# Two state-space convolutions and two feed-forward layers on one core: first load of h, warm-up, last store and instruction order changed

## The chip, the cores and the metric

The kernel runs on one core of a Trainium2 chip. The metric is the device time of one execution in microseconds; the verdict of a comparison is the median over several executions.

## The reference

Two layers, each a convolution block A and a feed-forward block B, on 2048 rows of 512 columns in bfloat16. `q` is the running `x`, and each block is added to it.

```python
def _A_ref(q, k, v, shift_k, ssm_k, ssm_D):           # q is layernorm(x)
    k_shift = sum over t of k_pad[:, t:t + S, :] * shift_k[:, ks - 1 - t]   # 4 taps along the rows
    kv = k_shift * v
    y = irfft(rfft(kv, 2S) * rfft(ssm_k, 2S))[:S]     # causal convolution along the rows, 2048 long
    return q * (y + kv * ssm_D)
def _B_ref(x, w_gate, w_up, w_down):                  # x is layernorm(x); 512 -> 1792 -> 512
    return (silu(x @ w_gate) * (x @ w_up)) @ w_down
x = A_q
x = x + A(layernorm(x)); x = x + B(layernorm(x))      # twice, with the same weights
```

## The kernel before

The 2048 rows are cut into four chunks of 512 (`c` = 0 to 3), each laid out as 128 partitions times four rows. The convolution of each chunk works on spectra of length 1024: matmuls with cosine and sine tables (`fwd`) make the spectra `X` of `k_shift * v` and `H`, `G` of the filter, VectorE multiplies them into `Z`, and matmuls with the transposed tables (`inv`) bring them back as `Y`. The taps of `k` are matmuls with diagonal matrices `dg`. `prologue` multiplies `Y` with the normalised `x`, adds, normalises again and turns the result into `zT`. `ffn` runs one unit of 256 rows: gate and up matmuls of 256 columns into PSUM tiles `pf` (line 311), silu and copy on ScalarE into `sg` and `ht` (lines 970 and 974), their product on VectorE (line 977), and the down matmuls into `pd` (line 990). There are 16 units; `LAST_UNIT` is the last.

Nothing is issued as the code stands. `add` records each operation with its engine, a cost, and its predecessors; `Plan.order` sorts the recorded operations by a table of numbers, `ORDER`, written out by hand, and works out starts from the costs and from the latencies (`lat`) given to transfers. `Plan.issue` emits them in that order on the five engines. Where PE would sit idle in the first 32 us by these starts, `issue` puts warm-up matmuls `wm` there through `warm`: so many as fit in the hole at 0.106 us each. They write to a free PSUM buffer and nothing reads them. Each engine keeps its list in order, so that an operation waits behind all that stand ahead of it.

The start goes like this. On ScalarE's queue the taps (`tapR`) and `ssm_D` (`drow`, line 1069, after VectorE's memset of line 1053) are loaded, then the table load and the two `Sin` activations that make `fwd` (line 1105). On SP's queue stand `hn` (`load_h`, the first 512 columns of the filter), `kn` (`load_k`), `vt` (`load_v`), `xc` (`load_x`), the next `hn` and `vt`, and the gate weights. PE turns `hn` (`transpose_h`, line 477) and `kn` (`transpose_k`, line 366); ScalarE and VectorE copy them out as `hs` and `kTb` (lines 487, 490, 493, 372, 374). Spectra of `h` are the eight first matmuls of line 311, copied out as `ev`; `G` follows from `ev` (lines 445 and 447).

`ln_stats_act` takes the sums of a layer norm on ScalarE (lines 828 and 834, with the row sums accumulated beside) for eight of the 32 norms; its last operation on that engine makes `ve`, the variance with the epsilon, which GpSimd raises to the power of -0.5. `ln_stats` does the same with VectorE's `bn_stats` (line 809) and its `ve` on VectorE (line 812).

The last row of the last unit is split by columns into two halves, so that VectorE adds one half (line 1008) and SP stores it while ScalarE copies the other (line 1011) and its own queue stores that (line 1014). For the second half `x` itself is added in PSUM by a matmul with the identity (line 949).

Of the kernel before, what the change touches and what calls it, by code (L numbers as in the profile page):

```python
# [30 lines left out]
LK0 = 4.3  # L31
# [11 lines left out]
H_SPLIT = False  # L43
# [7 lines left out]
LASTV = True  # L51
ORDER = [
# [186 lines left out]
def kernel(  # L239
# [1024 lines left out]
    def warm(ring, slot, n):  # L1264
        t = psp.tile([P, P], F32, name="wm", tag=f"{ring}{slot}")
        for _ in range(n):
            nc.tensor.matmul(t[:], lhsT=wz.t[:], rhs=wz.t[:], start=True, stop=True)  # L1267
# [33 lines left out]
```

## Time and profile before

| what | value |
|---|---|
| time, median of 3 runs | 346.92 us (344.28 to 723.23) |
| the profiled execution: time, span from first to last instruction | 344.93 us, 343.2 us |
| PE busy | 336.4 us (98%), 2579 matmuls |
| PE weight loads | 248.6 us (72%) |
| VectorE busy | 283.4 us (83%), 482 instructions |
| ScalarE busy | 253.9 us (74%), 504 instructions |
| GpSimd busy | 35.3 us (10%) |
| first gate matmul starts | 33.58 us |
| last copy out of PSUM starts | 340.00 us |
| mean granted clock | 1.000 |

Busy time of PE is modelled from starts and does not tell whether matmuls run at full rate; the distance from start to start does. A line of the timeline has the start in microseconds from the first instruction, the duration of the whole group, the engine, the line of the code, what is written from what, the shape and the count, and in brackets the idle time before with what ended it.

### The profile page before, as it was taken

The numbers are of one execution on the slowest core, as the hardware profiler recorded it, in microseconds if no ns is written. First come the engines' busy times: TensorE is split into PE (matmuls) and PEld (weight loads), VectorE is DVE, ScalarE is ACT, GpSimd is POOL, SyncE is SP. The second block draws the span as 40 slices with busy tenths as digits, with TensorE's granted clock in tenths as the row PEclk, the third lists the DMA queues.
The fourth block names the chain that finished last, engine by engine and source line by source line (L and its number), as shares of the span: only waits on it lengthen the run. The fifth ranks groups of instructions, "written<-read, shape, count | busy, mean of one in ns | idle before, by whom it ended". The sixth has DMA issues, their size and how long they took to land.

```text
span 343.2 us, 6553 instructions
## 1 busy us (share of the span) xinstructions
PE 336.4 (98%) x2579; PEld 248.6 (72%) x2610; DVE 283.4 (83%) x482; ACT 253.9 (74%) x504; POOL 35.3 (10%) x46
## 2 busy tenths in 40 slices
PE   8999999999999999999999999999999999999996
PEld 7756868768687676858586777768685877777783
DVE  8899999899999999899999999989998433726022
ACT  6999999899997765958789995779475464446261
POOL 4010100203111000103110100201101001000000
PEclk9999999999999999999999999999999999999999
DMA  7999218310116044040101014210101100110101
GB/s 273 336 316 341 52 27 112 77 32 0 34 31 94 14 95 138 2 94 3 32 2 46 2 46 79 76 32 1 32 0 33 35 13 0 39 39 8 24 26 37
DMA packets 42088, 22.95 MB, mean 67 GB/s; under 512 B 33861, under 2 KB 39882, under 8 KB 42058
## 3 DMA queue, kind: packets, MB, share of 16 engines
q1 hardware_dynamic: 41904, 22.47, 26.6%
q8 instruction: 20, 0.33, 0.4%
q14 instruction: 10, 0.08, 0.1%
q10 hardware_dynamic: 154, 0.07, 0.1%
HBM read 12.33 MB, written 2.10 MB: 42 GB/s over the span
## 4 chain that ended last, share of the span: by engine, by line
PE 91%; ACT 4%; DVE 3%; issue 1%
PE pf L311 54%; PE pd L990 28%; PE ps L311 6%; PE ps L458 1%; ACT H L419 1%; PE wm L1267 1%; DVE bnst L809 1%; ACT hs L487 1%; PE pt L477 1%; ACT X L419 0%; ACT n L859 0%; PE pt L366 0%; DVE m L540 0%; DVE t L665 0%; DVE Z L667 0%
## 5 line engine op out<-in xcount | busy, mean ns | idle before, releaser
L311 PE MATMUL pf<-zT,wu_sb 128*128 128x256 bf16 x896 | 110.4, 273 | 0.1
L311 PE MATMUL pf<-zT,wg_sb 128*128 128x256 bf16 x896 | 110.2, 273 | 0.2
L990 PE MATMUL pd<-wd_sb,ht 128*128 128x512 bf16 (+1 forms) x440 | 102.4, 372 | 1.2
L311 PEld LDWEIGHTS <-wu_sb 128*128 128x128 bf16 x896 | 87.7, 98 | 16.4
L311 PEld LDWEIGHTS <-wg_sb 128*128 128x128 bf16 x896 | 87.6, 98 | 16.5 <-issue 0.8
L974 ACT CAST ht<-pf 128x512 bf16<-128x512 f32 x112 | 64.0, 591 | 29.3 <-PE pf L311 29.1
L970 ACT ACTIVATE sg<-pf 128x512 bf16<-128x512 f32 x112 | 65.5, 603 | 17.4 <-PE pf L311 15.1
L990 PEld LDWEIGHTS <-ht 128*128 128x128 bf16 x462 | 45.2, 98 | 42.5
L977 DVE TENSOR_TENSOR ht<-ht,sg 128x1024 bf16<-128x1024 bf16 (+1 forms) x64 | 39.0, 617 | 24.0 <-ACT sg L970 18.7
L814 POOL TENSOR_TENSOR rstd<-ve,nhalf 128x2 f32<-128x2 f32 x24 | 23.0, 958 | 217.8 <-DVE ve L812 207.6
L1034 ACT CAST dn<-pd 128x512 bf16<-128x512 f32 x30 | 17.0, 589 | 21.0 <-PE pd L990 20.9
L809 DVE BATCH_NORM_STATS2 bnst<-xc 128x6 f32<-128x512 bf16 x48 | 31.6, 684 | 0.6
L419 ACT ACTIVATE X<-ps 128x512 bf16<-128x512 f32 x32 | 19.2, 611 | 4.0 <-PE ps L311 3.4
L653 DVE TENSOR_TENSOR t<-X,G 128x2048 bf16<-128x2048 bf16 x18 | 21.9, 1218 | 0.1
L657 DVE TENSOR_TENSOR t<-X,G 128x2048 bf16<-128x2048 bf16 x18 | 21.9, 1216 | 0.0
L1037 DVE TENSOR_TENSOR xc<-xc,dn 128x1024 bf16<-128x1024 bf16 x15 | 10.3, 689 | 13.4 <-ACT dn L1034 13.2
L665 DVE TENSOR_TENSOR t<-t,t 128x2048 bf16<-128x2048 bf16 x12 | 14.7, 1222 | 0.3
L667 DVE TENSOR_TENSOR Z<-Z,t 128x2048 bf16<-128x2048 bf16 x12 | 14.6, 1220 | 0.2
L840 POOL TENSOR_TENSOR rstd<-ve,nhalf 128x2 f32<-128x2 f32 x8 | 8.7, 1088 | 59.2 <-ACT ve L838 59.1
L419 ACT ACTIVATE H<-ps 128x512 bf16<-128x512 f32 x24 | 13.8, 610 | 0.1
L886 DVE TENSOR_TENSOR n<-n,Yk 128x1024 bf16<-128x1024 bf16 x15 | 10.3, 688 | 4.1 <-ACT n L859 3.8
L604 ACT ACTIVATE kc<-kTb,tapF 128x512 bf16<-128x512 bf16 x16 | 12.1, 783 | 0.0
(105 smaller groups left out, 323.3 us busy)
## 6 DMA issues: line engine op xcount, KB each, us to landing
hn<-in_A_ssm_k_dram SPq DMA_DIRECT2D x4, 512.0 KB, 4.1
vt<-in_A_v_dram SPq DMA_DIRECT2D x4, 512.0 KB, 5.9
xc<-in_A_q_dram SPq DMA_DIRECT2D x4, 512.0 KB, 5.3
out_dram<-xc SPq DMA_DIRECT2D x15, 128.0 KB, 1.8
wg_sb<-in_B_w_gate_dram SPq DMA_DIRECT2D x1, 1792.0 KB
wu_sb<-in_B_w_up_dram SPq DMA_DIRECT2D x1, 1792.0 KB, 8.5
wd_sb<-in_B_w_down_dram SPq DMA_DIRECT2D x1, 1280.0 KB, 12.0
kn<-in_A_k_dram SPq DMA_DIRECT2D x1, 512.0 KB, 4.5
```

Source lines behind the costliest of these rows:

```text
L311: nc.tensor.matmul(o, lhsT=lhsT, rhs=rhs, start=(n == 0), stop=(n == len(terms) - 1))
L419: add("ACT", act(D), lambda: nc.scalar.activation(out=view(), in_=ps.t[:], func=ACT.Copy, scale=scale), r=[ps], w=[(buf, keys)], conv=conv)
L653: dve(n * D, lambda t1=t1, part=part: nc.vector.tensor_mul(out=t1.t[:], in0=x.t[:, sl, 0, :], in1=g.t[:, sl, part, :]), [(x, key(slots, (0 ...
L657: dve(n * D, lambda t2=t2, part=part: nc.vector.tensor_mul(out=t2.t[:], in0=x.t[:, sl, 1, :], in1=g.t[:, sl, 1 - part, :]), [(x, key(slots ...
L665: dve(n * D, lambda t1=t1, t2=t2, comb=comb: nc.vector.tensor_tensor(out=t1.t[:], in0=t1.t[:], in1=t2.t[:], op=comb), [t2], [t1], conv=conv)
L809: add("DVE", 0.6, lambda st=st, i=i: nc.vector.bn_stats(out=st.t[:], in_=xs[c].t[:, i, :]), r=[(xs[c], (i,))], w=[st])
L814: add("POOL", pw, lambda: nc.gpsimd.tensor_tensor(out=rstd.t[:], in0=ve.t[:], in1=nhalf.t[:].to_broadcast((P, n)), op=ALU.pow), r=[ve, nha ...
L970: add("ACT", act(D), lambda ps=ps, o=o, sg=sg: nc.scalar.activation(out=sg.t[:, o:o + 2, :], in_=ps.t[:], func=ACT.Silu), r=[ps], w=[(sg, ...
L974: add("ACT", act(D), lambda ps=ps, o=o, ht=ht: nc.scalar.copy(out=ht.t[:, o:o + 2, :], in_=ps.t[:]), r=[ps], w=[(ht, (o // 2,))], due=(uni ...
L977: dve(n * W, lambda sg=sg, ht=ht: nc.vector.tensor_mul(out=ht.t[:], in0=ht.t[:], in1=sg.t[:]), [sg], [ht], due=(unit, k / pairs, 0.0, "h"))
L990: nc.tensor.matmul((pds[o] if not cs.start else pds[HP]).t[:, cs], lhsT=ht.t[:, q, o * P:(o + 1) * P], rhs=wt["d"].t[:, ft, cs], start=(ft ...
L1034: add("ACT", act(D), lambda o=o: nc.scalar.copy(out=dn.t[:, o, :], in_=pds[o].t[:]), r=[pds[o]], w=[(dn, (o,))], due=(unit, 1.0, 3.0, "h"))
```

## The change

1. `H_SPLIT` is now true: the first `hn` is loaded by two transfers of two blocks each, the second recorded after the first, both ahead of `kn` on SP's queue. PE's transposes of it are then recorded by halves, each waiting for its own transfer.
2. The warm-up matmuls read the framework's constant tile of ones; the tile `wz` and its memset are gone. The number of matmuls in a hole is counted without the 0.3 us that was left free, where the hole begins after 0 and before 8 us, and from 0 for the first one. There are 37 in place of 31: 25 before the taps, 6 between `h` and `k`, 6 ahead of the transposes of `z`.
3. The last row is cut at column 320: VectorE and SP take 320, ScalarE and its queue 192.
4. `ve` in `ln_stats_act` is made by VectorE (`VE_D`): eight operations move.
5. The latencies given to the first `k`, `v` and `x` loads are smaller; they steer the planner's starts alone.
6. `ORDER` is another table throughout. Of what the change speaks of, the lists then stand as follows. PE: 25 `wm`, the four transposes of the taps, 6 transposes of the first half of `h`, 10 that need the second, 6 `wm`, all 16 of `k`, 8 spectrum matmuls (before: 22 `wm`, taps, 5 `wm`, 16 of `h`, 8 of `k`, 8 spectrum matmuls, 8 of `k`). VectorE: `nhalf`, one `ph`, then the memset of `drow`; all eight of its `dg` before its two `kTb` copies. SP: the second `xc` behind both parts of `wd_sb`, where it stood between them.

```diff
-LK0 = 4.3
+LK0 = 3.8
-H_SPLIT = False
+H_SPLIT = True
+TAIL = 320
+VE_D = True
 ORDER = [
...
-                            n = int((start - max(t, 0.3) - 0.3) / 0.106)
+                            n = int((start - t - (0.0 if 0.0 < t < 8.0 else 0.3)) / 0.106)
...
         if b == 0 and H_SPLIT:
+            o = None
             for n in range(2):
                 sl = slice(2 * n, 2 * n + 2)
                 o = add(eng, 0.5, lambda sl=sl: q.dma_start(out=hn[b].t[:, sl], in_=h3[:, sl, 0:L]), w=[(hn[b], (n,))],
-                        lat=LH0 - 0.75 if n == 0 else LH0 - 0.45, due=due, after=after)
+                        lat=(2.95, 3.1)[n], due=due, after=[o] if n else after)
...
-lat=(6.6, 9.0)[b] if b < 2 else 5.5
+lat=(5.7, 8.6)[b] if b < 2 else 5.5
-lat=(7.5, 13.0, 5.0, 5.0)[c]
+lat=(6.2, 13.0, 5.0, 5.0)[c]
...
-        add("ACT", TINY, lambda: nc.scalar.activation(out=ve.t[:], in_=sm.t[:, n:2 * n], func=ACT.Identity, scale=1.0 / D, bias=eps.t[:]),
-            r=[(sm, range(n, 2 * n)), eps], w=[ve])
+        if VE_D:
+            add("DVE", 0.08, lambda: nc.vector.tensor_scalar(out=ve.t[:], in0=sm.t[:, n:2 * n], scalar1=1.0 / D, scalar2=LN_EPS,
+                                                             op0=ALU.mult, op1=ALU.add), r=[(sm, range(n, 2 * n))], w=[ve])
...
-                halves = (slice(0, D // 2), slice(D // 2, D)) if unit == LAST_UNIT and o == HP - 1 else (slice(0, D),)
+                halves = (slice(0, TAIL), slice(TAIL, D)) if unit == LAST_UNIT and o == HP - 1 else (slice(0, D),)
...
-            for half_, (eng, cs) in enumerate((("DVE", slice(0, D // 2)), ("ACT", slice(D // 2, D)))):
+            for half_, (eng, cs) in enumerate((("DVE", slice(0, TAIL)), ("ACT", slice(TAIL, D)))):
...
-    wz = whole("wz", [P, P])
-    add("DVE", 0.07, lambda: nc.vector.memset(wz.t[:], 0.5), w=[wz], due=-80)
+    ones = nc.const_aps.tensor(1.0, (P, P), BF16)
...
-            nc.tensor.matmul(t[:], lhsT=wz.t[:], rhs=wz.t[:], start=True, stop=True)
+            nc.tensor.matmul(t[:], lhsT=ones, rhs=ones, start=True, stop=True)
```

More of the change, by code (lines that the diff above doesn't have):

```diff
@@ L381, in load_v @@
             return add("ACT", 0.45, lambda: nc.scalar.dma_start(out=vt[b].t[:], in_=v_t[:, b]), w=[vt[b]], lat=5.5, due=-69.5, after=[h0])
-        return add("SP", 0.6, lambda: nc.sync.dma_start(out=vt[b].t[:], in_=v_t[:, b]), w=[vt[b]], lat=(6.6, 9.0)[b] if b < 2 else 5.5, due=due, after=after)
+        return add("SP", 0.6, lambda: nc.sync.dma_start(out=vt[b].t[:], in_=v_t[:, b]), w=[vt[b]], lat=(5.7, 8.6)[b] if b < 2 else 5.5, due=due, after=after)
     def load_x(c, due=None, after=()):
         xs[c] = new("x", "xc", [P, R, D], parts=R + 2)
-        return add("SP", 0.7, lambda: nc.sync.dma_start(out=xs[c].t[:], in_=q_t[:, c]), w=[xs[c]], lat=(7.5, 13.0, 5.0, 5.0)[c], due=due, after=after)
+        return add("SP", 0.7, lambda: nc.sync.dma_start(out=xs[c].t[:], in_=q_t[:, c]), w=[xs[c]], lat=(6.2, 13.0, 5.0, 5.0)[c], due=due, after=after)
     def load_weights(which, due, after=()):
@@ L837, in ln_stats_act @@
         ve, rstd = new("ve", "ve", [P, n], F32), new("rs", "rstd", [P, n], F32)
-        add("ACT", TINY, lambda: nc.scalar.activation(out=ve.t[:], in_=sm.t[:, n:2 * n], func=ACT.Identity, scale=1.0 / D, bias=eps.t[:]),
-            r=[(sm, range(n, 2 * n)), eps], w=[ve])
+        if VE_D:
+            add("DVE", 0.08, lambda: nc.vector.tensor_scalar(out=ve.t[:], in0=sm.t[:, n:2 * n], scalar1=1.0 / D, scalar2=LN_EPS,
+                                                             op0=ALU.mult, op1=ALU.add), r=[(sm, range(n, 2 * n))], w=[ve])
+        else:
+            add("ACT", TINY, lambda: nc.scalar.activation(out=ve.t[:], in_=sm.t[:, n:2 * n], func=ACT.Identity, scale=1.0 / D, bias=eps.t[:]),
+                r=[(sm, range(n, 2 * n)), eps], w=[ve])
         add("POOL", PWA, lambda: nc.gpsimd.tensor_tensor(out=rstd.t[:], in0=ve.t[:], in1=nhalf.t[:].to_broadcast((P, n)),
@@ L982, in ffn @@
                 split = unit == LAST_UNIT and o == HP - 1
-                halves = (slice(0, D // 2), slice(D // 2, D))
+                halves = (slice(0, TAIL), slice(TAIL, D))
                 cols = [[cs] for cs in halves] if last else [halves] if split else [[slice(0, D)]]
@@ L991, in go @@
                                                  start=(ft == 0 and not own(o, cs)), stop=(ft == NF - 1))
-                    add("PE", pe(n) if not last else pe(n, D // 2), go, r=[ht, (wt["d"], (0 if fts[0] == 0 else 1,))],
+                    add("PE", pe(n) if not last else pe(n, css[0].stop - css[0].start), go, r=[ht, (wt["d"], (0 if fts[0] == 0 else 1,))],
                         w=[pds[o]] if not split else [pds[o], pds[HP]] if not last else [pds[HP if css[0].start else o]],
@@ L1004, in ffn @@
                 due=(unit, 1.0, 20.0, None))
-            for half_, (eng, cs) in enumerate((("DVE", slice(0, D // 2)), ("ACT", slice(D // 2, D)))):
+            for half_, (eng, cs) in enumerate((("DVE", slice(0, TAIL)), ("ACT", slice(TAIL, D)))):
                 copy = nc.scalar.copy if eng == "ACT" else nc.vector.tensor_copy
                 if LASTV and not half_:
-                    add(eng, 0.35, lambda cs=cs: nc.vector.tensor_add(out=x.t[:, i, cs], in0=x.t[:, i, cs], in1=pds[o].t[:, cs]),
+                    add(eng, 0.42, lambda cs=cs: nc.vector.tensor_add(out=x.t[:, i, cs], in0=x.t[:, i, cs], in1=pds[o].t[:, cs]),
                         r=[pds[o], (x, (i,))], w=[(x, (R + half_,))], due=(unit, 1.0, 3.0, "h"))
                 else:
-                    add(eng, 0.35, lambda cs=cs, copy=copy, half_=half_: copy(out=x.t[:, i, cs], in_=pds[HP if half_ else o].t[:, cs]),
+                    add(eng, 0.3, lambda cs=cs, copy=copy, half_=half_: copy(out=x.t[:, i, cs], in_=pds[HP if half_ else o].t[:, cs]),
                         r=[pds[HP if half_ else o]], w=[(x, (R + half_,))], due=(unit, 1.0, 3.0, "h"))
```

116 rows, old and new, of the table ORDER are left out of this document.

## The prediction

> **What bounds the kernel now.** I read the page's slices first, then PE's waits over the whole span, then the order of time at both ends.
>
> ```profile
> span 343.2 us, 6553 instructions
> PE   8999999999999999999999999999999999999996
> DVE  8899999899999999899999999989998433726022
> PEclk9999999999999999999999999999999999999999
> ```
>
> The second list is the waits of PE: who released it, then us in total, times, longest.
>
> ```profile
> PE wm L1267 <- DVE wz L1050: 1.0, 1, 1.0
> PE ps L311 <- ACT H L419: 0.4, 1, 0.4
> PE ps L311 <- DVE vt L515: 0.4, 1, 0.4
> ```
>
> The two waits for `H` and `vt` fall at 24 and 31 us. The first gate matmul (`pf`) starts at 33.58 us, and PE waits for nothing it could be given after that. The chain shows the rate:
>
> ```profile
> 303.27 10.48 PE pf L311 x96
> 317.23 3.45 PE pd L990 x16
> ```
>
> That is 109 ns per 256 columns and 216 ns per 512. From 33.58 us to the last matmul at about 340 us TensorE runs one matmul after the other at that rate, so a new order can gain nothing there; it can only open holes. What can be gained lies ahead of 33.58 us and behind 340 us. First column start, second duration:
>
> ```profile
> 0.72 0.45 SPq L342 DMA_DIRECT2D hn<-in_A_ssm_k_dram  x1
> 0.82 0.17 DVE L1050 MEMSET wz<- 128x128 bf16 x1 [0.82 <-PEq L1285]
> 1.04 2.53 PE L1267 MATMUL wm<-wz 128*128 128x128 bf16 x22 [1.04 <-DVE wz L1050]
> 1.24 0.48 SPq L352 DMA_DIRECT2D kn<-in_A_k_dram  x1
> 3.50 0.29 PE L1133 MATMUL pt<-ident,tapR 4*128 4x4 bf16 x4
> 4.49 1.86 PE L477 MATMUL pt<-ident,hn 128*128 128x128 bf16 x16
> 6.15 1.06 PE L366 MATMUL pt<-ident,kn 128*128 128x128 bf16 x8
> 8.87 0.61 PE L366 MATMUL pt<-ident,kn 128*128 128x128 bf16 x8
> ```
>
> Sixteen transposes of `h` take 1.86 us, each starting 107 ns after the one before; the second eight of `k` start 56 ns apart. So TensorE runs at half its clock until the first columns of L311 at about 7.3 us and at full clock from then on. The PEclk row shows 9 throughout and hides this; the spacing is the measure.
>
> Work ahead of 33.58 us at full rate: 48 transposes of `h` and `k`, 8 of `z` and 128 matmuls of `dg` at 56 ns are 10.3 us, 74 matmuls of 512 columns at 216 ns are 16.0 us, together 26.3 us. From 4.49 us that would end at 30.8. So 2.8 us are lost there: 24 transposes at 107 in place of 56 ns (1.2 us), a half-rate matmul (0.1), the two waits (0.8), and small steps. VectorE matters just as much: its idle times in that stretch are these, and from 10 us on it has almost none.
>
> ```profile
> DVE kTb L374 <- PE pt L366: 1.2, 2, 0.6
> DVE G L447 <- ACT ev L419: 0.4, 1, 0.4
> ```
>
> **The change, part by part.**
>
> First `h` in two transfers: one more SP issue of 0.45 us. The first half, 256 KB, cannot land sooner than a 4 KB transfer nor later than the whole: `tapR`, issued at 0.72, is used at 3.49 (2.8 us), the whole `h` lands 3.6 us after issue. That is 3.5 to 4.3 us; I take 3.7. PE's list does six transposes of the first half, then ten that need the second. The second half is issued at about 1.2; its bytes are behind the same bytes as before, so I take 4.3, with 4.8 (3.6 after its own issue) as the late end. The ten at 107 ns then end at 5.5 (6.0 late) where 6.2 was the end: 0.2 to 0.7 us earlier. `k`, `v`, `x` and all else on SP's queue are issued 0.45 us later; `k` landed 4.5 us after issue, at 5.7, and would land at 5.7 if its bytes wait for those of `h` anyway, at 6.2 if not.
>
> Between `h` and `k` stand six warm-up matmuls that wait for nothing: 0.64 us at half clock. So `k` starts at 6.15 at half clock whatever its landing, no earlier than now; but all 16 transposes run in one go. With the clock up at 7.3 us as now, 11 of them run at 107 ns and five at 56, to 7.6 us, and the eight L311 matmuls behind them end at 9.3; now the same work ends at 9.48. That is 0.15 us. With the clock up at 4.5 us, `h` would end at 5.0, `k` (landed at 5.7) at 6.7, and the eight at 8.5: 1.0 us.
>
> Warm-up on the framework's ones: the `wz` memset (0.17 us) goes and PE starts at about 0.8, where the 0.82 us wait ends, not at 1.04. The 0.2 us gap after the warm-up closes. One trace shows one rise, 6.2 us after the first matmul; 0.2 us earlier by that row, up to 2.8 us by the bound above (none of the work before 4.5 us matters). The Trainium skill (TensorE: Matmul & The Clock Gate, Part 1) says that the clock rises at the end of a free-running window of about 3.4 us that was busy; by it the rise would come anywhere from about 4.2 to 7.6 us, by luck, and the front's gain would vary by up to 1 us from run to run. No single trace can show that.
>
> VectorE ahead of the first `pf`: all eight of its `dg` builds (299 ns each) now stand before the `kTb` copies, where it waited 0.6 us twice for PE. Total work is nearly equal: `wz` out (0.17), one `ve` in (0.17 by L812's 168 ns). If the waits of 1.2 and 0.4 us shrink by half, `z` and with it the first `pf` come 0.8 us earlier; if PE's 0.15 us is all that passes on, 0.15. Also `drow`'s memset moves behind the first `ph`, some 0.45 us later; ScalarE's `drow` DMA waits for it and the table load (1.28 us) stands behind that. ScalarE had 0.74 us idle before its first `hs` copy, which hides it; without that cover it costs up to 0.4. I take 0.6 us gained at the front; bounds 1.6 us gained, 0.4 lost.
>
> `ve` from ScalarE to VectorE: eight operations of 296 ns leave ScalarE, eight of 168 ns come to VectorE, 1.3 us. ScalarE's 2.4 us lie beside other work. VectorE is at eight tenths or more, mostly nine, up to some 240 us, so its 1.3 us has no certain cover; behind each `ve` stand the `ht` products (L977), and PE waits for those. Cost: nothing while PE's list has other matmuls to do, at most 1.3 us.
>
> The order anew: 28 matmuls of 256 columns become 14 of 320 and 14 of 192, the same columns; the rest of PE's matmuls is the same in kind and count. SP's list is the same but for places: the second `xc` load goes behind the last part of `wd`. A hole would show where none is now. Lower bound 0; upper bound by the largest wait that the present order leaves PE beyond the start, 0.4 us, a few times: 2 us. I take 0.2 for this and the `ve` together, as the present order of the same kind has none after 33.58.
>
> The last row. At the end stand these:
>
> ```profile
> 339.78 0.42 DVE L1008 TENSOR_TENSOR xc<-xc,pd 128x256 bf16<-128x256 bf16 x1 [0.40 <-PE pd L990]
> 340.00 0.37 ACT L1011 CAST xc<-pd 128x256 bf16<-128x256 f32 x1 [4.12 <-PE pd L990]
> 340.40 0.38 ACTq L1014 DMA_DIRECT2D out_dram<-xc  x1
> ```
>
> ScalarE's copy goes from 256 to 192 columns; 512 took 0.59, so 0.31 us, ending 0.06 earlier. VectorE's 320 columns (512 took 0.69) need 0.49 and start 0.05 later: they end at 340.32, about with the other. The end moves by 0.05 us; bounds 0.1 either way.
>
> Sum against the profiled execution, 344.93 us (span 343.2 and 1.7 around it): -0.6 + 0.2 - 0.05 is -0.45, so about **344.4 us**. That execution lies 2 us under the median of the runs shown, 346.92, and 0.7 over the lowest.
>
> **The rivals.**
>
> *The front's gain stops at VectorE.* For: VectorE is full from 10 us on and its work to `z` is not less. Against: 1.6 us of its waits lie before that. Then 0.1 to 0.2 us remain, and with the 0.2: 344.9.
>
> *The `ve` operations make VectorE the bound.* In the middle, up to 240 us, a `ht` product is late because 0.17 us per `ve` stands ahead, and PE, which keeps its order, stops. It decides once the delay exceeds the slack of the next L990 group. Against: the chain runs back through VectorE from 163 to 152 us, yet PE had no wait there. Price up to 1.3 us with no gain kept at the front: 346.2, slower than before.
>
> *The clock rises early.* Rise by 4.5 us and the VectorE waits gone: 1.6 us at the front, 343.3.
>
> *Transposes do not keep the clock up.* Between 3.9 and 7.3 us PE had five warm-up matmuls and 24 transposes, and the rise came at the end of it, which speaks against. If only matmuls counted, the 32 transposes now in a row would put the rise off to some 11 us: 16 of `k` at 107 ns and eight L311 at twice 216 ns, ending at 11.3 where it is 9.48, so 1.8 us more: 346.7. The Trainium skill says so of transposes (the same page, Part 4: PE-mode transpose); the trace disagrees.
>
> **How the numbers follow.** Forecast 0.53, gain lost at VectorE 0.2, VectorE the bound 0.11, early clock 0.08, transposes 0.04. Range 342.7 to 346.8: from the early clock with a little more to both slower cases. All lie within 2% (6.9 us), about what a measurement of this kernel can tell from no change. Beyond it there is only what I have no row for: a long hole in the new order, 0.03; faster 0.01.
>
> **What would show it.** Right: L477 starts at about 3.8; the transposes of `k` in one run; DVE's wait L374 on L366 under 0.6 us; first `pf` at 32.6 to 33.4; PE without waits after it. Wrong: `pf` at 33.6 or later, or waits of PE for `ht` or `zT` of over 1 us together in the middle. A time over 347 or under 342.5 would need a mechanism that I do not have.

## The result, and the profile after

The changed kernel is slower, by 0.7 to 1%. Its median is 348.1 us (22 executions, 344.67 to 351.79), that of the kernel before 344.44 (22 executions). The ratio given, here and below, leaves out executions more than 1.5% above the fastest of the same kernel, here five; the other 17 have a median of 347.31 and a ratio of 1.0067 [1.0049, 1.0085]. The forecast was 344.4, with a range up to 346.8. The profiled execution took 347.31 us (span 345.5), that of before 344.93 (span 343.2): 2.38 us to explain.

The slices of the span of the changed kernel, and PE's waits over the whole span (who released it; us in total, times, longest):

```profile
span 345.5 us, 6567 instructions
PE   6999999999999999999999999999999999999996
DVE  6699999999999999999999999999997344637022
PEclk9899999999999999999999999999999999999999
```

```profile
PE pt L369 <- DMA kn<-in_A_k_dram: 2.1, 1, 2.1
PE wm L1273 <- PEq L1291: 0.8, 1, 0.8
PE ps L313 <- issue: 0.2, 1, 0.2
PE ptz L927 <- DVE z L871: 0.2, 1, 0.2
```

The two waits of 0.4 us for `H` and `vt` are gone, as the new order wants. In their place stands one of 2.1 us for `k`, which was not there before. The row of the granted clock has an 8 in its second slice, where before it had 9 throughout. The start, from the timeline of the changed kernel, and the windows by stage (PE busy, PEld, DVE, ACT, POOL, then the granted clock, the DMA share and GB/s):

```profile
0.72 0.97 SPq L342 DMA_DIRECT2D hn<-in_A_ssm_k_dram  x2
0.76 2.83 PE L1273 MATMUL wm<-const-bfloat16-1.0 128*128 128x128 bf16 x25 [0.76 <-PEq L1291]
1.74 0.99 SPq L355 DMA_DIRECT2D kn<-in_A_k_dram  x1
3.73 1.61 PE L480 MATMUL pt<-ident,hn 128*128 128x128 bf16 x16
5.18 0.51 PE L1273 MATMUL wm<-const-bfloat16-1.0 128*128 128x128 bf16 x6
7.80 1.66 PE L369 MATMUL pt<-ident,kn 128*128 128x128 bf16 x16 [2.10 <-DMA kn<-in_A_k_dram]
9.25 1.06 PE L313 MATMUL ps<-hs,fwd 128*128 128x512 bf16 x2
36.31 1.03 PE L313 MATMUL pf<-zT,wg_sb 128*128 128x256 bf16 x8
```

```profile
4.00:8.00 4.00, 1.88 (x26) 1.44 (x24) 2.76 (x13) 3.03 (x7) 2.44 (x4) 1.00 0.94 331
8.00:12.00 4.00, 3.78 (x23) 2.37 (x22) 1.29 (x2) 3.02 (x8) 0.00 (x0) 0.57 1.04 397
```

`h` is there at 3.73 us and its transposes end at 5.34, 1.0 us before those of the kernel before. Then six warm-up matmuls run, and PE stands until 7.80. By the clock's own records it rose at 4.68 us, fell at 8.09 and rose again at 11.51: from 8 to 12 us TensorE had a mean granted clock of 0.57, just when the long row of work began. The first `pf` starts at 36.31 us in place of 33.58.

From there on the change does well. The last matmul starts 305.75 us after the first `pf` (before: 306.11), and the end is as forecast:

```profile
342.18 0.49 DVE L1015 TENSOR_TENSOR xc<-xc,pd 128x320 bf16<-128x320 bf16 x1 [0.46 <-PE pd L997]
342.34 0.32 ACT L1018 CAST xc<-pd 128x192 bf16<-128x192 f32 x1 [5.39 <-PE pd L997]
342.69 0.39 ACTq L1021 DMA_DIRECT2D out_dram<-xc  x1
```

From the last matmul's start to the end of the span are 3.42 us, before 3.46 (spans of 345.48 and 343.15 us to two digits). So the difference is +2.73 at the front, -0.36 in the middle and -0.04 at the end: +2.33 of span. The other 0.05 lies around the span. Ten of the 22 executions had a mean granted clock of 0.995 or less, as this one; six had 0.999 or 1.000 and still took over 348 us, and of those none was profiled. A mean of 1.000 does not say that the start was good: the clock's records begin at the first rise, and what lies ahead of it does not count. The kernel before has 1.000 with a rise at 7.28 us, and a run further below 348.86 us and 1.000 with a rise at 13.52.

### The profile page after: what moved, and what is told of

Read it like the earlier page. It is cut to its first block, busy times and chain, and to the rows that moved or that the text cites. A ratio compares the mean times of both kernels' runs of the same rounds, so it can differ in the third digit from the quotient of the medians.

```text
span 345.5 us, 6567 instructions
## 1 busy us (share of the span) xinstructions
PE 337.4 (98%) x2585; PEld 248.5 (72%) x2616; DVE 283.4 (82%) x489; ACT 250.5 (73%) x496; POOL 38.9 (11%) x46
## 4 chain that ended last, share of the span: by engine, by line
PE 89%; DVE 6%; DMA 2%; issue 1%; ACT 1%; SPq 0%; POOL 0%
PE pf L313 56%; PE pd L997 27%; PE ps L313 6%; DMA kn<-in_A_k_dram 2%; DVE t L645 1%; DVE Z L649 1%; DVE m L794 1%; DVE bnst L812 1%; PE pt L369 0%; DVE ht L984 0%; DVE Z L560 0%; ACT sg L977 0%; ACT ht L981 0%; SPq L342 0%; POOL rstd L817 0%
## 5 line engine op out<-in xcount | busy, mean ns | idle before, releaser
L997 PE MATMUL pd<-wd_sb,ht 128*128 128x512 bf16 (+2 forms) x441 | 101.4, 373 | 1.2
L817 POOL TENSOR_TENSOR rstd<-ve,nhalf 128x2 f32<-128x2 f32 x24 | 24.7, 1031 | 206.8 <-DVE ve L815 187.7
L847 POOL TENSOR_TENSOR rstd<-ve,nhalf 128x2 f32<-128x2 f32 x8 | 10.6, 1327 | 69.1 <-DVE ve L842 69.1
L313 PE MATMUL ps<-hs,fwd 128*128 128x512 bf16 x38 | 13.7, 408 | 0.3 <-issue 0.2
```

Of the source, the lines that this page charges most:

```text
L313: nc.tensor.matmul(o, lhsT=lhsT, rhs=rhs, start=(n == 0), stop=(n == len(terms) - 1))
L817: add("POOL", pw, lambda: nc.gpsimd.tensor_tensor(out=rstd.t[:], in0=ve.t[:], in1=nhalf.t[:].to_broadcast((P, n)), op=ALU.pow), r=[ve, nha ...
L997: nc.tensor.matmul((pds[o] if not cs.start else pds[HP]).t[:, cs], lhsT=ht.t[:, q, o * P:(o + 1) * P], rhs=wt["d"].t[:, ft, cs], start=(ft ...
```

## The experiments

The profile left two theories. **A:** the second transfer of `h` makes `k` land late, and the hole that this leaves in TensorE's work brings the clock down. **B:** one of the other edits (warm-up on ones, `ve`, the new order, `drow`'s later load) costs the time, and `k` is an accident of one execution. A number from the traces goes with each run: when `k` has landed. A transfer reports its landing in sixteen parts, and PE needs all of them; the number is the time of the last. It was 5.71 us before and 7.75 us after. The sixteen themselves say more. Before, they came between 5.13 and 5.71. In the changed kernel eleven are there by 5.82 us, though `k` was issued 0.50 later; the last five straggle in from 6.04 to 7.75.

**One transfer of `h`, the rest of the change kept.**

```diff
-                o = add(eng, 0.5, lambda sl=sl: q.dma_start(out=hn[b].t[:, sl], in_=h3[:, sl, 0:L]), w=[(hn[b], (n,))],
+                o = add(eng, 0.5, (lambda: q.dma_start(out=hn[b].t[:], in_=h3[:, :, 0:L])) if n == 0 else (lambda: None), w=[(hn[b], (n,))],
```

> The changed kernel with the first h in one transfer again; PE's list keeps its two halves, and all else stays. It moves k's issue forward by one SP issue (0.45 us or more), and since one transfer fewer is ahead of it, the small drow transfer on ScalarE's queue gets a completion lane of its own and no longer waits for the taps to land. Theory A (k lands late, PE stands idle in its place, and the clock falls for it): k lands at 5.7 to 6.3 us in place of 7.75, the wait for it falls from 2.1 to under 0.6 us, the clock does not fall, the first gate matmul starts at 33.2 to 34.0 in place of 36.31, time within 0.5 us of the kernel before. Rival B (ScalarE starts 1.7 us late because drow waits for the taps): the same gain, with the table load at about 1.6 us; the next run tells the two apart. Rival C (the new order or the moved ve costs the time): still 346.5 to 347.5.

Measured: 344.03 us, ratio to before 0.9996 [0.9978, 1.0015]. `k` landed at 5.43 us, its transposes began at 5.99, the clock rose once at 5.41 and stayed, and the first `pf` came at 32.83 us; the span was 342.0. All that the change lost comes back with this one line. Theory A holds for the size of the loss; as this edit also lets `drow`'s load start earlier, it does not yet exclude that part of B.

**The split kept, `drow`'s memset and load put back early.** In `ORDER` the ranks of the two were moved to the front.

> The changed kernel with the memset of drow and its transfer moved ahead in the order table, the transfer recorded between the two halves of h. It then has a lane of its own, and ScalarE's table load starts at about 1.6 us in place of 3.25. The split of h stays. Theory A: k lands as late as in the changed kernel (7 to 8 us), PE waits for it, the time stays 2 to 3 us above the kernel before. Rival B: the first gate matmul at 33.5 to 34.5, time within 0.7 us of the kernel before. Rival C: no change.

Measured: 345.63 us, 1.0043 [1.0016, 1.0070]. In the profiled execution `k` landed at 6.11, `pf` came at 33.01 and the clock stayed up; three of the other executions were at 347.0 to 348.5 us with a mean granted clock of 0.995 or 0.99, as in the changed kernel. A window of 3.41 us at half clock in a span of 345 is 0.5%, so 0.995 marks one such window. Theory A had wanted 7 to 8 us for `k` and 2 to 3 us over the kernel before; it was 1.1 us over. The interval overlaps with that of the changed kernel, so the times do not tell what the early load brings; the formula further below does.

**The change with 20 more warm-up matmuls between `h` and `k`.**

```diff
+                            if 2.0 < t < 8.0 and start < 12.0:
+                                n += 20
```

> The changed kernel with 20 more warm-up matmuls between the transposes of h and those of k, 1.1 us at full clock or 2.1 at half. k lands as before, so that its lateness stays, but PE stands idle for about 1 us in place of 2.1. Theory A, with the clock's fall as a part of the cost: the clock stays up in the runs in which it had risen by then, the eight first L313 matmuls run 216 ns apart in place of 430, and the time falls by 1 to 1.5 us against the changed kernel, to 345.5 to 346.5. If the lateness of k alone is the cost: no gain, or a loss of up to 1 us where the clock is still down and the fill ends after k has landed. Rivals B and C: no gain.

Measured: 346.0 us, 1.0053 [1.0032, 1.0073]. `k` was late again (7.06 us), but all eight executions had a mean clock of 0.999 or more (in the changed kernel 11 of 22, with the early `drow` 7 of 10). So the fall of the clock comes from the hole, and filling it removes the fall; the lateness of `k` stays and costs by itself.

**The kernel before with the split alone.**

```diff
-H_SPLIT = False
+H_SPLIT = True
...
-                        lat=LH0 - 0.75 if n == 0 else LH0 - 0.45, due=due, after=after)
+                        lat=(2.95, 3.1)[n], due=due, after=after)
```

`ORDER` got the entries for the second transfer and for the transposes by halves; `drow`'s load stays early.

> The kernel before with one part of the change alone: the first h in two transfers, PE's transposes by halves as in the changed kernel; its order, its warm-up and its drow transfer (ahead of k, on its own lane) stay. Theory A: k lands 0.5 to 2 us later than 5.7; the transposes of k start at 6.1 to 7.7 in place of 6.15; the time is up by 0.5 to 2 us, 345 to 346.5. If the split of h does not delay k: h done 0.5 us earlier, time within 0.3 us of the kernel before. Rivals B and C: within 0.3 us.

Measured: 347.45 us, 1.0077 [1.0051, 1.0103]: the whole loss without any other part of the change. PE's wait stands in its profile too, and the clock fell from 7.88 to 11.29 us:

```profile
PE pt L365 <- DMA kn<-in_A_k_dram: 2.4, 1, 2.4
```

This run and the three above ran on one chip, so that the chip is no explanation: `k` at 5.43 us with one transfer, at 6.11, 7.06 and 8.10 with two. Theory B has fallen as the cause of the loss.

What is it in the split that delays `k`? The DMA traffic between 3 and 4 us, first with one transfer of `h`, then in the kernel before with the split (packets, MB, and their time as a share of 16 engines):

```profile
DMA packets 264, 0.42 MB, mean 420 GB/s; under 512 B 16, under 2 KB 210, under 8 KB 264
...
q1 hardware_dynamic: 264, 0.42, 110.4%
```

```profile
DMA packets 229, 0.25 MB, mean 252 GB/s; under 512 B 16, under 2 KB 218, under 8 KB 229
...
q1 hardware_dynamic: 229, 0.25, 94.2%
```

The DMA engines are nearly as busy, but move 0.25 in place of 0.42 MB (0.39 in the kernel before, 0.27 in the changed one). The packets of `h` have 1024 bytes, those of `k` 4096. By the packet records the 4096-byte ones that start in this stretch take 159 ns on average with one transfer, 474 with two (before 162, the changed kernel 303); the small ones take 46 to 53 ns in all of them. The mean hides single packets: with one transfer all 54 took 159 ns, with two the longest of 11 took 835. Four runs asked why.

**A further issue ahead of `k`, with `h` in one transfer:** 512 bytes are loaded between the two into a tile that nothing reads, and `drow` is early.

```diff
+lambda: (nc.sync.dma_start(out=const.tile([1, 256], BF16, name="scr")[:], in_=A_ssm_D.rearrange("(o d) -> o d", o=1)[:, 0:256]),
                 nc.sync.dma_start(out=kn[b].t[:], in_=k_t[:, b]))
```

> The changed kernel with h in one transfer, the drow transfer early (own lane), and a transfer of 512 bytes that nothing reads on SP's queue between h and k. It delays the issue of k by one SP issue as the split does, and leaves the bytes and pieces of h as they were before. If the issue itself makes k late: k lands 1 to 2.5 us later than the 5.43 of the run with one h, PE waits for it, time 1 to 3 us over the kernel before, some runs with a fallen clock. If k is late because h is in two pieces: k lands at 5.4 to 6.0 and the time is within 0.5 us of the kernel before.

Measured: `k` landed at 6.03 us although it was issued as late as in the changed kernel, and its packets of 3 to 4 us took 159 ns. So the later issue is not what delays `k`. The time was 347.61 us all the same, 1.0088 [1.0054, 1.0122], and no theory had that; in three of the four executions the mean clock was 0.995 or less. The profiled one was the slowest, 349.39. In it `h` landed at 4.77 us (4.11 in the run with one `h`), and there was a second thing, at 38 us. Its lines, in order of time, of GpSimd, VectorE, ScalarE and PE:

```profile
38.42 4.20 POOL L847 TENSOR_TENSOR rstd<-ve,nhalf 128x2 f32<-128x2 f32 x1 [6.49 <-DVE ve L842]
38.58 2.36 DVE L584 TENSOR_TENSOR G<-H,G 128x2048 bf16<-128x2048 bf16 x2
40.85 1.22 DVE L656 TENSOR_TENSOR t<-X,G 128x2048 bf16<-128x2048 bf16 x1
42.66 0.48 ACT L859 ACTIVATE nmr<-nm,rstd 128x1 f32<-128x1 f32 x2 [2.76 <-POOL rstd L847]
45.07 1.62 PE L312 MATMUL pf<-zT,wu_sb 128*128 128x256 bf16 x8 [2.31 <-ACT ht L981]
```

GpSimd's `rstd`, 0.80 us at the same place in the run with one `h`, took 4.20 and ended 0.55 us after VectorE's last long product. ScalarE's `nmr` waited for it with the `ht` copies behind, PE waited 2.31 us for those, and the clock fell from 45.35 to 48.76. The Trainium skill (SBUF — State Buffer, SBUF: two separate sides) says that VectorE and GpSimd share a port pair as an exclusive lock, held for the whole instruction. The trace fits that: in the run with one `h` other `rstd` took 1.5 us or 2.67, and those too ended 0.55 us after a long product of VectorE, the first or the second that ran beside them. It adds that GpSimd did not get in between three products in a row. Why it waited here and not in the run with one `h`, where the first product began just as soon after it (0.16 us), is not shown.

**The split kept, `k` on ScalarE's queue**, `drow` early.

```diff
-            return add("SP", 0.5, lambda: nc.sync.dma_start(out=kn[b].t[:], in_=k_t[:, b]), w=[kn[b]], lat=LK0, ...)
+            return add("ACT", 0.5, lambda: nc.scalar.dma_start(out=kn[b].t[:], in_=k_t[:, b]), w=[kn[b]], lat=LK0, ...)
...
-        k0 = load_k(0, -69.9, after=[h0])
+        k0 = load_k(0, -69.9, after=[tr])
```

> The changed kernel with the split of h kept and k issued on ScalarE's queue, right behind the taps, at about 1.3 us; drow's transfer stands behind it and ScalarE's table load at about 2.1 us. The warm-up matmuls between h and k fall away, since the planner sees no hole there. If k is late by its place behind two transfers on SP's queue: k lands at 5.0 to 6.2, no wait over 0.4 us, no fallen clock, time 343.5 to 344.5. If splitting h slows k however k is queued: k lands after 6.5 and the time stays 1 us or more over the kernel before. The second half of h may land up to 1 us later than 4.5, as k's bytes now move beside it.

Measured: 346.42 us, 1.0073 [1.0044, 1.0102]. `k`'s packets of 3 to 4 us took 163 ns and `k` landed at 5.89, but now the packets of `k` and of `h`'s second half move at the same time: the halves of `h` came at 4.39 and 6.28 us, the transposes of `k` began at 7.38, and the clock rose at 9.10. In this profile another queue cures the slow packets and moves the lateness to `h`.

**The second half of `h` behind `k`**, `drow` early; PE's list as in the changed kernel.

> The changed kernel with ssm_D's load as early as before, and the second half of h issued behind k on SP's queue (the lists of TensorE stay, so it waits for that half ahead of k). A look at landings, not at the time. If k straggles because it stands right behind two transfers of h, it lands by 5.7 us here, with its 4096-byte packets of 3 to 4 us at about 160 ns each. If one short transfer of 256 KB ahead of it is enough, its packets take over 300 ns there and it lands after 6.2 us.

Measured: `k` landed at 5.58 us, its packets of 3 to 4 us took 168 ns. What stands behind the second half was slow instead: the 4096-byte packets that start between 5 and 6 us, those of `v`, took 443 ns. Here one half ahead was harmless, and the second was not. The time, 346.19 us in one execution, is that of PE waiting for the second half ahead of `k`.

**The split with a gap of one issue before `k`**, `drow` early.

> The changed kernel with ssm_D's load as early as before, and a transfer of 512 bytes between the second half of h and k, so that k is issued 0.45 us later, at about 2.2 us. A look at landings. If k straggles because it is issued close behind the second half, the gap cures it: packets of about 160 ns and a landing at 6.0 to 6.4 us. If two halves of h ahead are enough, it lands at 6.6 to 8.6 us, with packets over 200 ns.

Measured: no cure. `k` was issued at 2.15 us and landed at 8.64; its packets that start between 5 and 6 us took 365 ns. `k` started at 8.69, the clock rose at 13.52, and that one execution took 348.86 us.

So with two halves of `h` ahead of it on one queue `k` landed at 6.11 to 8.64 us (five runs), and at 5.43 to 6.18 us with one transfer of `h` or its first half ahead (seven runs, the later ones included; one profile each, and the ranges touch). In all five it is the later ones of the sixteen parts that make the difference: the earliest came between 5.23 and 5.50, with one transfer of all of `h` between 5.07 and 5.36. Why some packets behind the second half are slow, no run shows.

**The kernel before with the new warm-up alone.**

```diff
-    wz = whole("wz", [P, P])
-    add("DVE", 0.07, lambda: nc.vector.memset(wz.t[:], 0.5), w=[wz], due=-80)
+    ones = nc.const_aps.tensor(1.0, (P, P), BF16)
...
-                            n = int((start - max(t, 0.3) - 0.3) / 0.106)
+                            n = int((start - t - (0.0 if 0.0 < t < 8.0 else 0.3)) / 0.106)
```

> The kernel before with the warm-up alone changed: matmuls on the framework's ones, started at about 0.76 us in place of 1.04, 25 and 8 of them in place of 22 and 5. One h, its order and its copies stay. If the clock's rise comes with a window that is about three quarters busy, it comes 2.6 to 6.1 us after the first matmul, and in no run of this kernel does it fall again, since k is there when PE comes to it. Price: the 24 transposes and the matmuls behind them run at full rate in more of the runs; time 0.2 to 0.8 us under the kernel before. If VectorE and ScalarE hide it: no difference, within 0.3 us.

Measured: 344.49 us (344.23 to 344.83), 0.9995 [0.9982, 1.0007]: no difference in the median. In the profile the clock rose at 5.72 and `pf` came at 33.01 us.

**One `h`, `drow` early, no warm-up between `h` and `k`.**

```diff
+                            if 2.0 < t < 8.0 and start < 12.0:
+                                n = 0
```

> The changed kernel with h in one transfer, the drow transfer and its memset early, and no warm-up matmuls between h and k. ScalarE's table load starts at 1.6 us, k lands near 5.4 and its transposes start at 5.5 to 5.7 in place of 5.99 with the six fills. By theory A this keeps all that the rest of the change gains: first gate matmul at 32.2 to 32.9, time 0.3 to 1.0 us under the kernel before. If the six fills are what keeps the clock up: some runs with a fallen clock, and no gain.

Measured: 345.64 us, 1.0021 [1.0003, 1.0039], so the gain of 0.3 to 1.0 us did not come. In the profile `h` landed at 4.91, PE had stood 1.15 us before it, and the clock rose only at 8.77; `pf` came at 34.53.

**One `h`, and more warm-up on both sides of it:** six matmuls more between the taps and `h`, six more between `h` and `k`.

```diff
+                pe += 1
+                if pe == 2:
+                    warm("pd", 0, 6)
...
+                                n += 6
```

> The changed kernel with h in one transfer, and warm-up matmuls so that TensorE is never idle ahead of k: six more between the taps and h, six more between h and k. If a rise needs a window of 3.4 us that is about three quarters busy, and a fall one that is mostly idle, the rise comes between 3.3 and 6.8 us and nothing falls: first pf 32.6 to 33.2, time 343.4 to 344.0, all executions within 1 us. Rival: h and k are there before the extra twelve end (0.64 us each six at half clock), the front is later by 0.3 to 0.7 us: 344.4 to 344.8.

Measured: 345.77 us, 1.003 [1.0012, 1.0048]. The rival was right about the front: `k` had landed at 6.12, but its transposes began at 6.71, behind the filler, and `pf` came at 33.57, 0.74 us later than with one `h` alone. The time is 1 us above the rival's, and that lies elsewhere. From the first `pf` to the last matmul are 306.88 us, 1.14 more than with one `h` alone, and PE waits in that stretch for `zT`:

```profile
74.03 1.05 PE L318 MATMUL pf<-zT,wu_sb 128*128 128x256 bf16 x8 [0.96 <-DMA zT<-z]
```

Whether the filler brought that about, no run shows. The mean clock was 0.999 or more in all twelve executions, and eleven of them lie within 1.2 us.

**One `h`, and `ve` back on ScalarE:**

```diff
-VE_D = True
+VE_D = False
```

> The changed kernel with h in one transfer, as in the run with one h (344.03 us, 305.74 us from the first pf to the last matmul), and the eight `ve` back on ScalarE; the new order stays. If the moved `ve` costs nothing, both numbers stay within 0.3 us: 343.8 to 344.3, 305.7. If my price for it stands (up to 0.2 us), 305.5. Rival: the `ve` on VectorE stands right before VectorE's long products, and GpSimd's `rstd` behind it is held up in some executions (4.20 us in one profile in place of 0.8, with a hole of 2.3 us on TensorE): then the executions above 345 us go away and the median falls to 343.6.

Measured: 344.16 us, 0.9992 [0.9968, 1.0017]; 305.90 us from the first `pf` to the last matmul, where it is 305.74 with `ve` on VectorE. Five of the twelve executions lay above 345 us still (and some of the kernel before beside them), so the rival on `rstd` gets nothing from this. No cost of moving `ve` shows; a gain of 0.16 rests on one profile each.

No version was measurably faster than the kernel before. Three were the same within their intervals: the one with a single transfer of `h`, that with `ve` back on ScalarE too, and the kernel before with the new warm-up. The last row and the table of orders were not run alone.

**One formula for the front.** In all fourteen profiles the time from the first transpose of `k` to the first `pf` is 26.8 us plus half of the time that the clock was at half between the two:

| kernel | k landed | first transpose of k | at half clock until pf | pf | pf - start of k - half of that |
|---|---|---|---|---|---|
| before | 5.71 | 6.15 | 1.13 | 33.58 | 26.87 |
| after | 7.75 | 7.80 | 3.41 | 36.31 | 26.81 |
| one h | 5.43 | 5.99 | 0.00 | 32.83 | 26.84 |
| split, drow early | 6.11 | 6.15 | 0.00 | 33.01 | 26.85 |
| 20 more warm-up | 7.06 | 7.11 | 0.00 | 33.97 | 26.87 |
| before, split | 8.10 | 8.14 | 3.15 | 36.56 | 26.84 |
| one h, no warm-up | 6.18 | 6.64 | 2.12 | 34.53 | 26.82 |
| split, gap | 8.64 | 8.69 | 4.83 | 37.89 | 26.79 |

The other six lie between 26.81 and 26.88. Against the run with one `h`, the changed kernel loses 36.31 - 32.83 = 3.48 us: 1.81 by the later start of `k` and 1.71 by 3.41 us at half clock, 3.52 together. `drow`'s late load leaves no rest in it.

## Why the prediction was wrong, step by step

- **The failed step: "`k` [...] would land at 5.7 if its bytes wait for those of `h` anyway, at 6.2 if not".** It landed at 7.75. I had two ends, both from the issue time alone, and took the packets behind a split transfer to run as before. Between 3 and 4 us the traffic fell from 0.39 to 0.27 MB, and of the sixteen parts of `k` five were late. The cause of the slow packets stays open. "`k` starts at 6.15 [...] whatever its landing" was then false by 1.65 us: six warm-up matmuls covered only what I had expected.
- **The clock.** I had considered when it rises, not that it falls. In the window from 4.68 to 8.09 us PE worked from 4.68 to about 5.7 and from 7.80 on, 38% of it, and lost the clock for the next 3.41 us. The Trainium skill (TensorE: Matmul & The Clock Gate, Part 1) gives 3.4 us as the length of a free-running window; every fall here lasted 3.41 us, and the trace agrees. The rival that transposes do not keep the clock up does not hold: in the run with no warm-up between `h` and `k` the clock rose at the end of the window from 5.36 to 8.77 us, and PE did nothing but transposes in it until 8.35.
- **VectorE's waits.** "If the waits of 1.2 and 0.4 us shrink by half": the one for `k`'s transposes was 1.3 us in the changed kernel. By the formula the time from `k` to `pf` was the same with the old order and the new. What I credited to VectorE, 0.6 us, came in the run with one `h` as 0.75, from an earlier `k` and clock.
- **`drow`.** I put its delay at 0.45 us. The table load began at 3.25 in place of 1.59, because with one transfer more on the list `drow`'s load waited for the taps to land. It cost nothing that the formula shows. With one `h` the table load began at 2.03, the 0.44 that I had worked out.
- **`ve` and the new order:** priced at +0.2, measured -0.36 from the first `pf` to the last matmul (306.11 to 305.75, one profile each; with one `h` alone 305.74). Neither rival on VectorE came true.
- **Right:** the first half at 3.7 us (first transpose 3.73), the ten transposes ending at 5.5 (5.34), PE from 0.8 us (0.76), the last row with VectorE 0.49 and ScalarE 0.31 (0.49 and 0.32) and the end by -0.05 (-0.04).
- **The base.** The sum started from one execution of 344.93 us, and 22 of them have a median of 344.44. Against that the forecast of 344.4 is no change at all: a front that gained nothing would have hit it by luck. Nor is 2% what a measurement here tells from no change: the intervals of the ratios are 0.25 to 0.7% wide.

Put the measured terms into the sum, 344.93 + 2.73 - 0.36 - 0.04 = 347.26, and the profiled 347.31 is there. The forecast of the front had the wrong sign because the landing of `k` was taken from a run with one transfer ahead of it.

## What to carry to other kernels

A transfer cut in two brought its first half earlier here, and cost the transfer behind it more than it brought; before splitting, ask what stands next on that queue and what it feeds. At the start of this kernel TensorE's clock was worth as much as its work: a hole of 2.1 us was paid with 1.7 us more at half clock. And a front with several engines may still follow one event: look for the landing whose distance to the first steady work is the same in every run.

## What the runs showed of the hardware that was not expected

- 4096-byte packets behind two transfers of 256 KB on one queue took 303 to 474 ns on average between 3 and 4 us (four runs), where they took 159 to 162 behind one transfer of 512 KB; with `k` on another queue they took 163. Single packets of up to 960 ns make the mean, and a part of the sixteen completions comes late, not all: five in the changed kernel, ten in the kernel before with the split.
- The clock's windows lie freely: the first rise came between 3.39 and 13.52 us in the fourteen profiles, always a multiple of 3.41 us from the later changes of the same execution. A window 38% busy lost the clock; one with a hole of 0.4 us (88% busy, the split with `drow` early) kept it. For the first rise the share alone does not decide clearly: the window that ended at 3.39 us, busy from 0.76 on (77%), was enough in the run with 20 more warm-up matmuls; that of the kernel before, from 0.45 to 3.87, was busy for 73 to 78% by how long the four small transposes of the taps are counted, and was not.
- GpSimd's power of a 128x2 tile took 0.69 us at the least. Beside VectorE's bf16 products of 128x2048 in a row it also took 1.5, 2.67 or 4.20 us, and then ended 0.55 us after the first, the second or the third of them. Which one lets it in, no run shows.
